# A softmax-by-polynomial step moved from VectorE to GpSimd, in an order planned with the cost of both engines' shared accesses

## The chip, the cores and the metric

The kernel runs on one core of a Trainium2 chip. A core has a matrix engine (TensorE, PE in the profile), a vector engine (VectorE, DVE), a scalar engine for exponentials (ScalarE, ACT), a general engine (GpSimd, POOL) and a queue engine (SyncE, SP) that here only starts DMAs. Each works through its own list of instructions in order; semaphores order the engines among each other. On-chip memory is SBUF, and PSUM (eight banks) for what TensorE writes. The metric is the device time in microseconds of one execution, the median of several runs.

## The reference

Two attention blocks share the input `x` (1 x 2048 x 512) and are mixed by a gate. Block A is softmax attention with 32 heads of 16 dimensions; block B is linear attention with a learned feature map.

```python
g = sigmoid((x * gate_w).sum(-1, keepdims=True))
# A: softmax attention, 32 heads, Dh = 16
scores = einsum("bhqd,bhkd->bhqk", q, k) * Dh ** -0.5
a = (softmax(scores) @ v) @ A_wo
# B: feature maps by softmax over 16 features, both signs
phi_q = concat(softmax(pq), softmax(-pq)); phi_k = concat(softmax(pk), softmax(-pk))
kv = einsum("bhsf,bhsd->bhfd", phi_k, v); z = phi_k.sum(s)
b = ((phi_q @ kv) / (phi_q @ z + 1e-6)) @ B_wo
return g * a + (1 - g) * b
```

Block A needs 32 x 2048 x 2048 exponentials. That is 2048 tiles of 128 x 512 (128 keys by 512 queries of one head).

## The kernel before, in words

**Tiles.** Four tiles (four heads that lie in the four quarters of TensorE's rows) are a pack, and there are 512 packs. Sixteen packs, one for each block of 128 keys, are a group: one accumulator bank in which the four heads' values and the sums of the exponentials (a column of ones beside the values) build up. Eight groups cover 512 queries.

**Two ways to an exponential.** Most tiles go the short way. TensorE makes the scores of three or two tiles at a time (`_qk`) into a ring of five PSUM banks, ScalarE makes the exponentials of the three or two with one instruction (`_exp`, line 1035) into 25 slots `ET`, and TensorE multiplies them with the values (`_pv`, line 1104). Other tiles, "away", are made by VectorE (`_vector_batch`). It makes 2 to the power of the scaled score by hand, for batches of up to five tiles, in six steps:

1. `v_bits`, line 883, once a tile: the scores of the tile, a bank of PSUM, are scaled and written as unsigned integers to `vt`, so that the bits hold exponent and fraction.
2. `_frac`, line 907, once a batch: one byte of every word of `vt` becomes a 16-bit fraction in `vf`.
3. `_line`, line 909: a linear form of `vf` in `vu`.
4. `_sq`, line 910: `vf` squared.
5. `_cube`, line 911: `vu` times `vf`.
6. `v_out`, line 893: `vt`, scaled, plus `vu`, written as 16-bit words that are the exponentials in bfloat16.

There are two buffers `vt`, one `vf` and three `vu`. The tiles are then multiplied with the values by TensorE, one at a time (`pvx`). `SHARES` says for each of the 32 groups how many of its tiles are away, and `_plan_vector` spreads them over the packs of the group by an integer division; the two tiles of each of the first two batches (`SOON`) come on top.

**The rest of the work.** VectorE also takes what TensorE made out of PSUM (projections of q, k and v, lines 703, 759, 783; block B's projections, lines 1252 and 1268; finished output rows, lines 1489 and 1541), turns each accumulator (line 1157), divides by the sum (lines 1161 to 1169), and makes block B's feature maps (lines 1306 to 1365). GpSimd only sets constants at the start; its last instruction begins at 25.84 us. SP starts the DMAs, among them eight small ones per q projection that spread heads (line 761).

**The order.** Nothing of the order is left to the engines. The kernel makes a list of operations (`Plan.op`) with an engine, a cost in microseconds, dependencies, a priority (often a date, counted in packs) and an earliest date. `Plan.order` walks through time, keeps when each engine is free, takes the operation that can start first (among those within 0.02 us the one of least priority), hands out spare PSUM banks (three beside the ring; one of them holds the accumulator), and adds filling matmuls on zeros (line 1113) where TensorE would be idle too long. The result is each engine's list; `emit` writes it with the semaphore waits that the dependencies need. So each engine's list is fixed by the costs in the code, and where the chip differs from them an engine waits at its list's head while what stands behind it waits too.

Names that matter for the change: `LEAD` (how many packs ahead of its first use a batch is due), `VPRIO`, `VREL`, `QDUE`, `K0`, `SK`, `Q0`, `SQ` (dates of batches, q projections, and block B's parts), `FIRST` and `LAST` (sizes of the first and last batches), `ENDS` (where the last group's away tiles lie), `OREL` (earliest date of the last outputs).

## Time and profile before

| | |
|---|---|
| time, median of 3 runs | 838.03 us (837.74 to 838.34) |
| profiled execution: span from first to last instruction | 836.5 us; the page has no other time of it |
| TensorE busy | 792.9 us (95%), of it fills 255.3 us |
| VectorE busy | 806.8 us (96%), 1050 instructions |
| ScalarE busy | 825.4 us (99%), of it exponentials 823.1 us |
| GpSimd busy | 8.0 us (1%), all within the first 26 us |
| granted TensorE clock | 1.000 |

How to read it: the page gives for each engine the time in which it worked on some instruction, as a share of the span. Its groups put together instructions of one line, engine and operation: the output, the input and their shapes, how many there were, the busy time and the mean duration of one in ns, and then how long the engine had been idle just in front of them and who ended that. Durations of neighbours on an engine can overlap a little, so count times mean can be more than the busy time. A row of the table of waits has who waited, for whom, and in total how long, how many times, and the longest.

### The profile page before, as it was taken

The page shows a single profiled execution, that of the slowest core. Times are in us where ns is not written, and L with a number is a line of the kernel's source. Part 1 is how long each engine was busy: PE and PEld are TensorE (multiplying, and loading weights), DVE is VectorE, ACT ScalarE, POOL GpSimd, SP SyncE. Part 2 cuts the span into 40 slices and gives each one's busy share as a digit, 9 for nine tenths or more (in the row PEclk, how much of TensorE's full clock was granted, in tenths as well). Part 3 has the DMA queues.
Part 4 walks back from the last instruction along what each step waited for, and adds up shares of the span by engine and source line. Part 5 has one row for each costly group of instructions (what it writes and reads, how often), then busy time and mean ns, then how long its engine had stood idle before and what let it go on. Part 6 is the DMA issues. An engine that isn't in the chain of part 4 may idle for free.

```text
span 836.5 us, 19540 instructions
## 1 busy us (share of the span) xinstructions
PE 792.9 (95%) x8711; PEld 263.0 (31%) x8753; DVE 806.8 (96%) x1050; ACT 825.4 (99%) x733; POOL 8.0 (1%) x15
## 2 busy tenths in 40 slices
PE   9999999999999999999999999999999999999998
PEld 4323333333232222232223322222322223222234
DVE  6999999999999999999999999999998999999994
ACT  7999999999999999999999999999999999999997
POOL 3000000000000000000000000000000000000000
PEclk9999999999999999999999999999999999999999
DMA  9500000000000000210003010003100003000000
GB/s 250 157 6 8 1 7 1 2 1 8 2 7 2 7 1 8 52 22 13 1 7 59 20 33 2 4 5 70 27 15 8 1 11 79 21 8 2 2 2 27
DMA packets 49027, 20.01 MB, mean 24 GB/s; under 512 B 38704, under 2 KB 48944, under 8 KB 48944
## 3 DMA queue, kind: packets, MB, share of 16 engines
q1 hardware_dynamic: 48272, 18.58, 9.4%
q8 instruction: 68, 1.11, 0.6%
q10 hardware_dynamic: 672, 0.20, 0.1%
q14 instruction: 15, 0.12, 0.0%
HBM read 6.31 MB, written 2.10 MB: 10 GB/s over the span
## 4 chain that ended last, share of the span: by engine, by line
ACT 92%; DVE 5%; PE 2%; DMA 0%; SPq 0%; issue 0%
ACT ET L1035 92%; DVE vt L883 1%; PE ps L984 0%; DMA qT<-qraw 0%; SPq L761 0%; PE ps L633 0%; DVE vu L893 0%; PE ps L1113 0%; DVE bq L1268 0%; DVE vt L1321 0%; DVE VB L1252 0%; DVE T L1157 0%; DVE vf L907 0%; DVE vu L911 0%; DVE vf L910 0%; DVE bq L1315 0%
## 5 line engine op out<-in xcount | busy, mean ns | idle before, releaser
L1035 ACT ACTIVATE ET<-ps 128x1536 bf16<-128x1536 f32 x728 | 823.1, 1397 | 1.7 <-PE ps L984 1.5
L984 PE MATMUL ps<-qT,kT 32*128 32x512 bf16 (+2 forms) x2249 | 318.4, 364 | 31.4 <-ACT ET L1035 22.2
L1113 PE MATMUL ps<-kT,zero 128*32 128x512 bf16 (+1 forms) x3052 | 255.3, 383 | 0.0
L1104 PE MATMUL ps<-ET,V 128*32 128x512 bf16 (+2 forms) x1998 | 195.8, 364 | 1.3 <-ACT ET L1035 0.6
L984 PEld LDWEIGHTS ps<-qT,kT 32*128 32x128 bf16 x2249 | 83.5, 91 | 305.5 <-ACT ET L1035 227.1
L883 DVE TENSOR_SCALAR vt<-ps 128x512 uint32<-128x512 f32 x226 | 148.3, 681 | 3.8 <-PE ps L984 3.1
L893 DVE SCALAR_TENSOR_TENSOR vu<-vt,vu 128x2560 int16<-128x2560 uint32 (+3 forms) x47 | 127.6, 2716 | 0.7
L1113 PEld LDWEIGHTS ps<-kT,zero 128*32 128x32 bf16 x3052 | 67.9, 94 | 103.2 <-issue 78.5
L1104 PE MATMUL ps<-vu,V 128*32 128x512 bf16 (+1 forms) x250 | 85.3, 364 | 0.3 <-DVE vu L893 0.3
L1104 PEld LDWEIGHTS ps<-ET,V 128*32 128x32 bf16 x1998 | 55.0, 95 | 67.0 <-issue 36.9
L910 DVE TENSOR_TENSOR vf<-vf 128x2560 f16<-128x2560 f16 (+3 forms) x49 | 68.6, 1400 | 0.6
L911 DVE TENSOR_TENSOR vu<-vu,vf 128x2560 f16<-128x2560 f16 (+3 forms) x49 | 68.5, 1398 | 0.5
L907 DVE TENSOR_SCALAR vf<-vt 128x2560 f16<-128x2560 uint8 (+3 forms) x47 | 67.1, 1427 | 0.2
L681 PE MATMUL ps<-WB,xT 128*128 128x512 bf16 x165 | 48.8, 383 | 4.0 <-issue 1.6
L909 DVE TENSOR_SCALAR vu<-vf 128x2560 f16<-128x2560 f16 (+3 forms) x49 | 37.9, 774 | 2.0 <-PE ps L1104 1.8
L681 PE MATMUL ps<-xT,WA 128*128 128x512 bf16 (+1 forms) x124 | 35.8, 380 | 0.0
L1157 DVE STREAM_TRANSPOSE T<-ps 128x512 f32<-128x512 f32 (+1 forms) x35 | 23.2, 664 | 5.0 <-PE ps L1104 4.6
L1104 PEld LDWEIGHTS ps<-vu,V 128*32 128x32 bf16 x250 | 22.9, 96 | 11.5 <-issue 8.5
L681 PEld LDWEIGHTS ps<-WB,xT 128*128 128x128 bf16 x192 | 14.4, 97 | 27.0 <-issue 14.3
L1268 DVE TENSOR_SCALAR bq<-ps 128x512 bf16<-128x512 f32 x32 | 21.5, 679 | 0.5 <-PE ps L681 0.4
L777 PE MATMUL ps<-WA,xT 128*128 128x128 bf16 x256 | 18.9, 220 | 0.4 <-DVE vt L883 0.2
L1321 DVE TENSOR_TENSOR vt<-vt,brec 128x4096 bf16<-128x4096 bf16 (+1 forms) x10 | 18.6, 1857 | 0.0
(105 smaller groups left out, 421.8 us busy)
## 6 DMA issues: line engine op xcount, KB each, us to landing
qT<-qraw SPq DMA_DIRECT2D x120, 16.0 KB, 1.8
xn<-in_A_x_dram SPq DMA_DIRECT2D x3, 512.0 KB, 6.1
WB<-in_B_wqkv_dram SPq DMA_DIRECT2D x3, 512.0 KB, 5.0
out_dram<-WB SPq DMA_DIRECT2D x12, 128.0 KB, 1.9
WA<-in_A_wqkv_dram SPq DMA_DIRECT2D x3, 384.0 KB, 5.2
xn<-in_A_x_dram SPq DMA_DIRECT2D x2, 256.0 KB, 3.6
WoA<-in_A_wo_dram SPq DMA_DIRECT2D x1, 512.0 KB, 5.7
WoB<-in_B_wo_dram SPq DMA_DIRECT2D x1, 512.0 KB, 6.6
```

What stands on the lines that cost most here:

```text
L681: mm = op("PE", lambda e, c=c: e.matmul(self._bank(job)[:, 0:n], lhs(c), rhs(c), start=(c == 0), stop=(c == 3)), self.c_pe(n), reads=reads ...
L883: parts.append(op("DVE", lambda e, j=j, job=job: e.tensor_scalar(vt[:, j, :], self._bank(job), SCALE * LOG2E * 2.0 ** 24, 2.0 ** 31, op0=A ...
L893: o = op("DVE", lambda e: e.scalar_tensor_tensor(out=flat(vu).bitcast(I16), in0=flat(vt), scalar=2.0 ** -17, in1=flat(vu), op0=ALU.mult, o ...
L907: ("_frac", two, lambda e: e.tensor_scalar(vf, frac, 1 / 256, ROOT, op0=ALU.mult, op1=ALU.add), [b_vt], [b_vf]),
L909: lambda e: e.tensor_scalar(vu, vf, CUBE, SQUARE, op0=ALU.mult, op1=ALU.add), [b_vf], [b_vu]),
L910: ("_sq", two, lambda e: e.tensor_tensor(vf, vf, vf, ALU.mult), [b_vf], [b_vf]),
L911: ("_cube", two, lambda e: e.tensor_tensor(vu, vu, vf, ALU.mult), [b_vf, b_vu], [b_vu]),
L984: ins = e.matmul(out[u][:, cols], self.kT[32 * i:32 * i + 32, cp, kt * TOK:(kt + 1) * TOK], self.qT[32 * i:32 * i + 32, s, q], start=True, ...
L1035: o = plan.op("ACT", lambda e: e.activation(self.ET[:, a % NS:a % NS + n, :], self.ps[:, a % NR:a % NR + n, :], ACT.Exp, scale=SCALE), sel ...
L1104: ins = e.matmul(self._bank(ot)[32 * i:32 * i + 32, to], self.V[:, kt, g8 // 2, v0:v0 + 32], tile[:, cols], start=first and j == 0, stop=o ...
L1113: ins = e.matmul(self._bank(ot)[32 * i:32 * i + 32, lo:QCH], self.zero[:], self.kT[:, 0, lo:QCH], start=False, stop=False, tile_position=( ...
L1157: return e.transpose(to, acc if alone else acc.rearrange("p (e b d) -> p e b d", e=2, b=8))
```

## The change

The fraction step (`_frac`) of the batches goes from VectorE to GpSimd, except in the first two batches (the `SOON` tiles) and the last two. There it is cut in pieces of at most three tiles: a batch of five is a piece of three and a piece of two. Each piece depends on the reads (`v_bits`) of its own tiles, on the last readers of `vf`, and on the `v_out` made last.

The planner gets a rule for what it calls the port: a set of names, which holds VectorE's steps between SBUF and SBUF (steps 2 to 6 above, block B's feature maps, parts of the division) and the pieces on GpSimd. An instruction of the set on one of the two engines doesn't begin before the other engine's last one of the set has ended, plus 0.1 us (GpSimd after VectorE) or 0.12 us (VectorE after GpSimd). VectorE doesn't start one that would begin less than 0.25 us before the next piece that GpSimd could start. Each such order becomes a dependency, hence a semaphore wait. VectorE's reads of PSUM aren't in the set. A piece's planned cost is 0.165 us and 0.00084 us per element.

TensorE may score into the banks for a tile buffer once `_cube` of the buffer's earlier batch is done, where it waited for the buffer's last reader; the read `v_bits` itself now waits for the last readers.

The shares are new (they add up to 246 where they added up to 226), the last group has ten away tiles where it had seven (spread over 11 places where it was 9). The rest batch stays in front of the last. Dates get a correction for each batch (`EASE`, `HURRY`), each q projection (`QEASE`), each part of block B (`LEASE`) and each output tile (`OEASE`), and several general dates are changed.

```diff
+        self.port = name in Plan.PORT
...
+    PORT = {"v_frac", "v_line", "v_sq", "v_cube", "v_out", "gate_z", "gate_h", "gate_b", "n_den", "n_mul", "kvbd", "b_grid", "b_rest",
+            "b_max", "b_top", "b_octave", "b_square", "b_slope", "b_even", "b_odd", "b_part", "b_out", "b_sum", "b_ratio", "b_mul"}
+    GUARD, GIVE, TAKE = 0.25, 0.1, 0.12
...
+            pool = [(max(free["POOL"], o.dep_t, port["DVE"].end + self.GIVE if port["DVE"] else 0.0), o) for o in avail["POOL"]
+                    if o.port and o.rel <= self.now]
+            booked = min(pool, key=lambda x: x[0]) if pool else None
...
+                    if o.port and e == "POOL" and port["DVE"]:
+                        t = max(t, port["DVE"].end + self.GIVE)
+                    elif o.port and e == "DVE":
+                        if port["POOL"]:
+                            t = max(t, port["POOL"].end + self.TAKE)
+                        if booked and t > booked[0] - self.GUARD:
+                            t = max(t, booked[0] + booked[1].cost + self.TAKE)
...
+            if o.port and e in port:
+                other = port["DVE" if e == "POOL" else "POOL"]
+                if other is not None:
+                    o.deps.append(other)
+                port[e] = o
...
-    QDUE, VPRIO, VREL, TPRIO = 28.0, -16.0, 161.0, 5
-    KEEP = 14
+    NVT, PIECE = 2, 3
+    QDUE, VPRIO, VREL, TPRIO = 32.287, -12.758, 161.0, 1
+    KEEP = 15
...
-    OREL = 3
-    ENDS = 9
+    OREL = 0
+    ENDS = 11
+    POOL = 0.00084
+    SOONER = "_cube"
+    TAIL = 2
...
-    SHARES = (0, 2, 2, 6, 0, 5, 4, 5, 8, 4, 9, 9, 10, 4, 15, 4,
-              2, 14, 8, 8, 12, 3, 6, 7, 14, 8, 7, 12, 6, 11, 14, 7)
+    SHARES = (0, 2, 4, 6, 2, 0, 5, 5, 16, 0, 9, 13, 4, 13, 11, 3, 11, 13, 6, 9, 9, 6, 12, 4, 11, 11, 8, 5, 12, 12, 14, 10)
...
-            due = max(units[0] / 4 - self.LEAD, self.EARLY if 2 * k >= len(soon) else self.SDUE)
+            due = max(units[0] / 4 - self.LEAD + self.EASE[k], self.EARLY if 2 * k >= len(soon) else self.SDUE)
...
-                   reads=self._score_bufs([u]), deps=b_vt.readers, name="vqk", prio=due + step * j, rel=due + step * j - self.VREL, kind="row",
+                   reads=self._score_bufs([u]), deps=b_vt.soon or b_vt.readers, name="vqk", prio=due + step * j, rel=due + step * j - self.VREL, kind="row",
...
-                op0=ALU.mult, op1=ALU.add), self.c_dve(512), deps=[m], name="v_bits",
+                op0=ALU.mult, op1=ALU.add), self.c_dve(512), deps=[m, *b_vt.readers], name="v_bits",
...
-        prio = units[0] / 4 - self.VPRIO
+        prio = units[0] / 4 - self.VPRIO + self.HURRY[number]
...
-            op("DVE", fn, cost, reads=reads, writes=writes, name="v" + name, prio=prio)
-        o = op("DVE", lambda e: e.scalar_tensor_tensor(
+            if name == "_frac" and not soon and number < len(self.batches) - self.TAIL:
+                o = self._frac(vt, vf, parts, b_vt, b_vf, prio)
+            else:
+                o = op("DVE", fn, cost, reads=reads, writes=writes, name="v" + name, prio=prio)
+            if name == self.SOONER:
+                b_vt.soon = [o]
+        self.last_out = o = op("DVE", lambda e: e.scalar_tensor_tensor(
...
+    def _frac(self, vt, vf, parts, b_vt, b_vf, prio):
+        free, made, at = b_vf.readers or b_vf.writers, [], 0
+        while at < len(parts):
+            n = min(self.PIECE, len(parts) - at)
+            made.append(self.plan.op(
+                "POOL", lambda e, a=at, n=n: e.tensor_scalar(
+                    vf[:, a:a + n, :], vt[:, a:a + n, :].bitcast(U8).rearrange("p n (q h) -> p n q h", h=4)[:, :, :, 2], 1 / 256, ROOT,
+                    op0=ALU.mult, op1=ALU.add), 0.165 + n * QCH * self.POOL, deps=[*parts[at:at + n], *free, self.last_out],
+                name="v_frac", prio=prio))
+            at += n
+        b_vt.readers += made
+        b_vf.writers, b_vf.readers = made, []
+        return made[-1]
...
-    K0, SK, Q0, SQ = 17.0, 8.5, 178.25, 18.0
+    K0, SK, Q0, SQ = 17.036, 8.76, 176.771, 19.0477
...
-            due = max(128 * (qc + 1) + 8, self.Q0 + self.SQ * (4 * qc + 4) + 22) + 4 * tt
+            due = max(128 * (qc + 1) + 8, self.Q0 + self.SQ * (4 * qc + 4) + 22) + 4 * tt + self.OEASE[t]
```

More of the change, by code (lines that the diff above doesn't have):

```diff
@@ L32, in __init__ @@
         self.readers = []
+        self.soon = []
 class Job:
@@ L81 @@
     LATE = 9.5
+    PORT = {"v_frac", "v_line", "v_sq", "v_cube", "v_out", "gate_z", "gate_h", "gate_b", "n_den", "n_mul", "kvbd", "b_grid", "b_rest",
+            "b_max", "b_top", "b_octave", "b_square", "b_slope", "b_even", "b_odd", "b_part", "b_out", "b_sum", "b_ratio", "b_mul"}
+    GUARD, GIVE, TAKE = 0.25, 0.1, 0.12
+    MOVE = {}
     def __init__(self):
@@ L94, in op @@
            acquire=None, release=None, lat=None, array=None, groups=None):
+        if name in self.MOVE:
+            eng, cost = "POOL", self.MOVE[name](cost)
         o = Op(eng, fn, cost, name, prio, rel, kind, self.LAT[eng] if lat is None else lat, groups)
@@ L165, in order @@
         queues = {e: [] for e in self.ENGS}
+        port = {"DVE": None, "POOL": None}
         left = len(self.ops)
@@ L383 @@
     LAST = (4,)
-    OREL = 3
-    ENDS = 9
+    OREL = 0
[3 more added lines that the diff above has]
+    TAIL = 2
+    REST = 48
+    HURRY = (0, 9.6, 3.1, -5.4, 16.2, -6.1, 0, -3.2, 10.5, 1.0, -8.4, 1.5, -3.1, 0.6, 12.0, 0, 9.6, 12.6, 0, -8.4, 6.7, 11.7,
+              7.3, 0.7, -7.6, 2.9, 0.1, 0, 3.9, 0.3, 13.7, 4.0, 0, 3.9, -14.1, -5.6, -2.1, 7.4, 4.3, -1.8, -2.7, 18.1, -9.4,
+              5.8, 4.8, 3.9, -6.0, 0, 0, 0, 0, 0, 0, 0, 0, 0, 0, 0, 0, 0)
+    QEASE = (0, 4.2, -1.3, -2.9, 5.7, 0.3, 9.3, 7.6, 5.5, 9.6, -1.4, -2.2, -1.6, 9.1, 3.3, 2.1)
+    LEASE = (-2.3, 3.2, 8.7, -2.0, 0, -20.0, -1.6, -2.5, -9.6, -3.3)
+    OEASE = (-0.2, -4.3, 8.5, -1.3, 2.6, -5.0, 14.2, -2.3, 10.6, -2.1, 6.7, 3.8, 0.9, 0, 0, 0)
+    EASE = (0, -0.9, 0, 6.0, -3.1, 3.7, 3.4, 3.9, 4.6, -1.9, -1.0, 0.1, 12, 8.0, 5.5, -12.1, -3.2, 8.6, 12, 9.8, 0, -1.0, -9.5,
+              -3.3, -14, 0, 9.6, -2.8, -0.4, -10.7, 0, 10.0, -8.8, 5.2, -5.7, -4.3, -10.6, 0, -0.6, -3.0, 9.6, 3.5, -3.4, 12,
+              12, -14, -4.8, 0, -0.2, 4.8, 0, -4.5, -1.6, 0, 0, 4.2, 0, 0, 0, 0)
+    NBANK = 8
     def __init__(self, nc, A_x, A_wqkv, A_wo, B_wqkv, B_w_phi, B_wo, gate_w, out):
@@ L403, in build @@
             p.pad = lambda ot: lambda e: self._fill(e, ot)
-            p.free_banks = [(b, 0.0, []) for b in range(self.NRING, 8)]
+            p.free_banks = [(b, 0.0, []) for b in range(self.NRING, self.NBANK)]
             self._loads()
@@ L439, in _memory @@
         self.xn = sb("xn", [P, NT, D], BF16)
-        at[0] = max(at[0], xn_at + 2 * self.NB * QCH * 4)
-        self.vt = nc.alloc_sbuf_tensor_at("vt", [P, 2, self.NB, QCH], I32U, offset=xn_at)
+        at[0] = max(at[0], xn_at + self.NVT * self.NB * QCH * 4)
+        self.vt = nc.alloc_sbuf_tensor_at("vt", [P, self.NVT, self.NB, QCH], I32U, offset=xn_at)
         self.xT = sb("xT", [P, NT, 4, TOK], BF16)
@@ L752, in _proj_q @@
         n = qc * 4 + cp
-        due = 32 * n - self.QDUE
+        due = 32 * n - self.QDUE + self.QEASE[n]
         s0 = 2 * (n % (self.NQS // 2))
@@ L844, in _plan_vector @@
         left = len(self.away) - sum(self.FIRST) - sum(self.LAST)
-        sizes = [*self.FIRST, *[self.NB] * (left // self.NB), *[left % self.NB] * (left % self.NB > 0), *self.LAST]
+        sizes = [self.NB] * (left // self.NB)
+        sizes[self.REST:self.REST] = [left % self.NB] * (left % self.NB > 0)
+        sizes = [*self.FIRST, *sizes, *self.LAST]
         ends = [sum(sizes[:k + 1]) for k in range(len(sizes))]
@@ L865, in _vector_batch @@
         NB = len(units)
-        k, slot, soon = self.n_bits % 2, number % self.NVU, 2 * number < len(self.SOON)
+        k, slot, soon = self.n_bits % self.NVT, number % self.NVU, 2 * number < len(self.SOON)
         self.n_bits += not soon
@@ L884, in _vector_batch @@
                 vt[:, j, :], self._bank(job), SCALE * LOG2E * 2.0 ** 24, 2.0 ** 31,
-                op0=ALU.mult, op1=ALU.add), self.c_dve(512), deps=[m], name="v_bits",
+                op0=ALU.mult, op1=ALU.add), self.c_dve(512), deps=[m, *b_vt.readers], name="v_bits",
                 prio=due + step * j - 40, release=job))
-        b_vt.writers, b_vt.readers = parts, []
+        b_vt.writers, b_vt.readers, b_vt.soon = parts, [], []
         self.last_bits = parts
         n = NB * QCH
-        prio = units[0] / 4 - self.VPRIO
+        prio = units[0] / 4 - self.VPRIO + self.HURRY[number]
         for name, cost, fn, reads, writes in self._cubic(flat(vt), flat(vf), flat(vu), n, b_vt, b_vf, b_vu):
-            op("DVE", fn, cost, reads=reads, writes=writes, name="v" + name, prio=prio)
-        o = op("DVE", lambda e: e.scalar_tensor_tensor(
+            if name == "_frac" and not soon and number < len(self.batches) - self.TAIL:
[5 more added lines that the diff above has]
+        self.last_out = o = op("DVE", lambda e: e.scalar_tensor_tensor(
             out=flat(vu).bitcast(I16), in0=flat(vt), scalar=2.0 ** -17, in1=flat(vu), op0=ALU.mult, op1=ALU.add),
@@ L918, in _attention @@
         self.n_bits = 0
+        self.last_out = None
         self._plan_vector()
@@ L925, in _attention @@
         self.b_outt = [Buf() for _ in range(6)]
-        self.b_vt, self.b_vf, self.b_vu = [Buf() for _ in range(2)], Buf(), [Buf() for _ in range(self.NVU)]
+        self.b_vt, self.b_vf, self.b_vu = [Buf() for _ in range(self.NVT)], Buf(), [Buf() for _ in range(self.NVU)]
         for b in self.b_vt:
@@ L1199, in _branch_b @@
             if t < self.PAIRS or t % 4 == 0:
-                due = self.K0 + self.SK * t
+                due = self.K0 + self.SK * t + self.LEASE[len(self.linear)]
                 self.linear.append((due, lambda t=t, due=due: self._b_keys(t, 2 if t < self.PAIRS else 4, due)))
         for t in range(0, NT, 4):
-            due = self.Q0 + self.SQ * t
+            due = self.Q0 + self.SQ * t + self.LEASE[len(self.linear)]
             self.linear.append((due, lambda t=t, due=due: self._b_queries(t, due)))
@@ L1274, in _b_part @@
             x.writers, x.readers = list(parts), []
-        k, n, h, ng = self.n_bits % 2, 2 * nt * QCH, nt * QCH, 16 * nt
+        k, n, h, ng = self.n_bits % self.NVT, 2 * nt * QCH, nt * QCH, 16 * nt
         self.n_bits += 1
         b_vt, b_vf = self.b_vt[k], self.b_vf
+        b_vt.soon = []
         two, four = lambda n: 0.057 + n * 0.000525, lambda n: 0.066 + n * 0.000262
```

## The prediction

> **What bounds the kernel now.** I read the engine totals first, then the costliest groups, then ScalarE's waits, then VectorE and GpSimd by shape, then VectorE in stretches of 50 us and in order of time. The head of the page and two of its groups:

> ```profile
> span 836.5 us, 19540 instructions
> PE 792.9 (95%) x8711; PEld 263.0 (31%) x8753; DVE 806.8 (96%) x1050; ACT 825.4 (99%) x733; POOL 8.0 (1%) x15
> ...
> L1035 ACT ACTIVATE ET<-ps 128x1536 bf16<-128x1536 f32 x728 | 823.1, 1397 | 1.7 <-PE ps L984 1.5
> ...
> L1113 PE MATMUL ps<-kT,zero 128*32 128x512 bf16 (+1 forms) x3052 | 255.3, 383 | 0.0
> ```

> ScalarE runs exponentials for 823.1 of 836.5 us and idles 1.7 us in front of them. The list of all that it ever waited for is short:

> ```profile
> ACT kT L721 <- PE ps L715: 3.7, 1, 3.7
> ACT xT L1544 <- PE ps L1531: 2.2, 1, 2.2
> ACT ET L1035 <- PE ps L984: 1.5, 3, 0.7
> ```

> (total, times, longest.) The exponentials start at 7.35 us, end at 831.64 us by order of time, and 4.9 us of last tile, eviction and store follow. So the time is a head, the exponentials and a tail: only fewer exponentials shorten it, as long as the others keep up. TensorE has room, by the table of waits:

> ```profile
> PEld ps L984 <- ACT ET L1035: 227.1, 510, 1.0
> PEld ps L1113 <- issue: 78.5, 324, 0.4
> ```

> It waits 227.1 us for ScalarE in front of the scores, and the 3052 matmuls of L1113 only fill. VectorE has hardly any: between 20 and 800 us its busy times by stretch add up to 768.7 of 780, 11.3 us idle. The granted clock is 1.00 in every stretch. VectorE's batch of five tiles, by shape (count | busy, mean ns):

> ```profile
> L883 DVE TENSOR_SCALAR vt<-ps 128x512 uint32<-128x512 f32 x226 | 148.3, 681 | 3.8 <-PE ps L984 3.1
> L893 DVE SCALAR_TENSOR_TENSOR vu<-vt,vu 128x2560 int16<-128x2560 uint32 x43 | 121.2, 2818 | 0.6
> L910 DVE TENSOR_TENSOR vf<-vf 128x2560 f16<-128x2560 f16 x43 | 63.7, 1482 | 0.5
> L911 DVE TENSOR_TENSOR vu<-vu,vf 128x2560 f16<-128x2560 f16 x43 | 63.6, 1479 | 0.4
> L907 DVE TENSOR_SCALAR vf<-vt 128x2560 f16<-128x2560 uint8 x43 | 63.6, 1478 | 0.2
> L909 DVE TENSOR_SCALAR vu<-vf 128x2560 f16<-128x2560 f16 x43 | 35.0, 813 | 2.0 <-PE ps L1104 1.8
> ```

> L907 is the step that moves. These durations overlap by about 0.08 us; what counts is the distance from start to start, read in order of time:

> ```profile
> 726.02 0.82 DVE L909 TENSOR_SCALAR vu<-vf 128x2560 f16<-128x2560 f16 x1
> 726.87 1.49 DVE L910 TENSOR_TENSOR vf<-vf 128x2560 f16<-128x2560 f16 x1
> 728.28 1.88 DVE L883 TENSOR_SCALAR vt<-ps 128x512 uint32<-128x512 f32 x3
> 730.08 1.48 DVE L911 TENSOR_TENSOR vu<-vu,vf 128x2560 f16<-128x2560 f16 x1
> 731.59 2.82 DVE L893 SCALAR_TENSOR_TENSOR vu<-vt,vu 128x2560 int16<-128x2560 uint32 x1
> ```

> That is 1.40 us for a product, 0.60 for one PSUM read of L883 (1.80 for three), 2.74 for L893 (start to next start), 0.74 to 0.85 for L909; L907 to its successor is 1.40 too.

> The sum is made against the profiled execution: its span of 836.5 us is all the page has of its own time; the median of the three runs, 838.03, stands 1.5 us above it, and I carry that 1.5 over.

> **The change, part by part.**

> *Tiles taken from ScalarE.* The shares add up to 226 before and 246 after, with 4 early tiles on top. But the formula of the places names a tile twice where a share is larger than the 14 places: a share of 15 in 14 before (one twice), 16 in 14 after (two twice). Distinct tiles: 229 before, 248 after. The trace agrees: 222 value matmuls of full width plus 7 last tiles in 4 blocks is 250, the count of L1104 from vu. ScalarE keeps 2048 - 248 = 1800 tiles instead of 1819: by shape it now has 364 threes, 363 twos and 1 one, afterwards 360 and 360. The planner's cost, 0.0642 us + 0.000833 per element, gives 822.8 us for what the row says is 823.1, so I use it: 4 threes (1.344), 3 twos (0.917) and 1 one (0.491) are **8.6 us less**. On the path in full, since the exponentials are the path.

> *VectorE's load.* Freed: L907 in all batches but the first two early ones and the last two: 43 x 1.40, and about 3.2 for the small ones, less 2.0 for the last batches of three and four that stay: 61.4 us. Added: 20 tiles (the second copies are made as well) of 0.60 for the read and (0.74 + 1.40 + 1.40 + 2.74)/5 = 1.26 for the rest: 37.1 us. Net 24.3 us freed. With the 11.3 us idle, and 8.6 us less span to do it in, VectorE can stand still for 27.0 us more than now before it is late: 49 batches go through GpSimd, so **0.55 us a batch**; 0.73 us a batch before the whole gain is gone (35.6/49).

> *GpSimd's pieces.* 47 batches of five in pieces of three and two, two batches of two: 96 pieces, at the end of a queue that is empty after 26 us. No trace shows this operation there. The nearest rows:

> ```profile
> L571 POOL MEMSET qT<- 128x2048 bf16 x1 | 1.8, 1804 | 0.0
> ...
> L574 POOL TENSOR_TENSOR wphi<-wphin,heads 128x512 bf16<-128x512 bf16 x1 | 1.1, 1051 | 1.5 <-DMA wphin<-in_B_w_phi_dram 1.5
> L791 POOL MEMSET gwb<- 128x544 bf16 x1 | 0.6, 631 | 0.0
> L1192 POOL MEMSET kvbd<- 128x544 bf16 x1 | 0.6, 552 | 0.0
> ```

> The memsets give 0.153 + 0.000806 per element (0.592 at 544, 1.804 at 2048): 1.39 and 0.98, 2.37 us a batch, as the low end (they read nothing). The product, with two inputs, has 2.05 ns an element: 3.15 and 2.10, 5.25 us, the high end. One input and a 2-byte output are nearest to the memset; the planner's 1.455 and 1.025, 2.48 us, lie beside it, and I take 2.48.

> *The waits that come with it.* A piece waits for the reads of its own two or three tiles, for the last L893 and, by the new rule of ports, for VectorE's last instruction of the port set; VectorE's next port instruction waits for the piece, and in its queue everything behind it does: the reads that free banks for TensorE, hence scores, hence ScalarE. A handover took 0.03 us in the trace (GpSimd's iden to VectorE's mask) and 0.06 (VectorE's onTA to TensorE); the planner's 0.1 and 0.12 are the upper bound: 2.48 + 0.22 = 2.70 us a batch. What hides it: instructions that read PSUM. The five L883 of another batch are 3.0 us, and they can start at the same L893 that lets the piece start. In all there are 148 us of L883 and, from their rows, some 147 of other non-port work (transposes, casts, evictions, reciprocals) against 49 x 2.70 = 132. If the cover holds, the cost is a few tenths a batch and inside the 0.55: nothing on the path. Bounds: 0 to 2.70 us a batch.

> *Scores released sooner, other dates.* TensorE may score for a tile buffer after the cube instead of L893; it takes a bank up to 2.7 us earlier and shortens the wait after L893. The 20 more single score and value passes are, with the planner's 0.213 and 0.104 for a switch, at most 12.7 us, in the place of fills (3052/4 x 0.213 = 163 us): nothing. The new dates of projections, branch B and stores, SP's 120 qT copies with them, move work that lies beside the exponentials; only head and tail could show it. The head has none of it; the last group has ten tiles instead of seven, and now two in the very last block, in the same batch of four that the block before needs: 0 to 1 us, taken as 0.

> *Sum.* 838.0 - 8.6 = 829.4; and 1.0 us for ScalarE's new small waits, an estimate: now 1.7 us with one supplier, and VectorE now has two sources of delay; between 0 and 4. **830.4 us.**

> **The rivals.**

> *VectorE waits for GpSimd (slower).* Two spare PSUM banks must turn over every 0.6 us to give five reads in a row; the longest run in the stretch shown is three (1.80 us), and elsewhere single reads lie between port instructions, which can't any more. With three as cover, a batch waits 2.70 - 1.80 = 0.90 us: 829.4 + 49 x (0.90 - 0.55) = **846.6**. It decides from 0.73 us a batch on. For it: 98.6% of VectorE is taken; between packs 256 and 384 the tiles go from 60 to 70, by which VectorE gains nothing (10 x 1.86 against 60 x 0.28). Against it: the work outside the port set, 295 us, is twice what is needed, and later tiles have slots for three batches. [...]

> *A part of the cover fails.* A wait of 0.65 us a batch: 829.4 + 49 x 0.10 = **834.3**, still faster.

> *GpSimd at the product's rate.* 5.47 us a batch with 3.0 covered: 829.4 + 49 x (2.47 - 0.55) = **923**. Against it: the step has one input.

> *ScalarE doesn't get shorter in effect:* the tiles go but dates misfit and ScalarE waits as long as it gained, **838**; for it only that VectorE's margin is small.

> **How the numbers follow.** Forecast case (827.5 to 832) 0.52; part of the cover 0.18; about as before 0.05; VectorE late 0.22 and GpSimd at the product's rate 0.03. What can be told from no change is about 0.2%, 1.7 us. Faster 0.70, same 0.05, slower 0.25. The low end is 829.4 less ScalarE's 1.7 us of waits, rounded: 827.5. Up to 842 the range takes in the partial case, no change and the mild third of the late case (a wait of 0.81 us a batch); what is left out above holds 0.18, below 0.03.

> **What would show it.** ScalarE: 720 exponentials, 814 us, waits below 5 us. GpSimd: 96 pieces near 1.45 and 1.0 us. VectorE: busy near 782 us, and waits on GpSimd below 27 us in all; if they pass 36 us, the forecast falls. If pieces last 2 us and more, the product's row was the right one. If ScalarE waits on TensorE while TensorE waits on VectorE's reads, the late case is here.

## The result and the profile after

The changed kernel takes 832.97 us, the median of four runs (830.17 to 833.76), against 838.18 us: a ratio of 0.9931 (95% interval 0.9915 to 0.9947). It is faster, by 5.2 us of the 7.6 that were forecast, and inside the range (827.5 to 842), which also held no change and a slower kernel. The profiled execution took 832.89 us, with a span of 831.0. In the head of its page and in its groups, the lines that answer to those of before (L1095 is the exponentials, L1173 the fills, L952 the pieces on GpSimd):

```profile
span 831.0 us, 19239 instructions
PE 799.8 (96%) x8526; PEld 263.4 (32%) x8526; DVE 785.8 (95%) x1041; ACT 817.2 (98%) x725; POOL 127.0 (15%) x111
...
PEclk9999999999979999999999999999999999999999
...
L1095 ACT ACTIVATE ET<-ps 128x1536 bf16<-128x1536 f32 x720 | 814.9, 1371 | 4.4 <-PE ps L1044 3.8
...
L1173 PE MATMUL ps<-kT,zero 128*32 128x512 bf16 (+1 forms) x2824 | 236.5, 386 | 0.0
```

Exponentials went from 823.1 to 814.9 us (728 to 720 instructions), ScalarE's idle time in front of them from 1.7 to 4.4 us. Those two account for the span: -8.2 + 2.7 = -5.5. The head (first exponential at 7.29 us, before 7.35) and the tail (4.9 us after the last one, as before) are the same.

GpSimd's pieces, by shape, and what VectorE waited for, by the table of waits (total, times, longest):

```profile
L952 POOL TENSOR_SCALAR vf<-vt 128x1536 f16<-128x1536 uint8 x47 | 69.2, 1471 | 605.0 <-DVE vu L938 360.7 <-DVE vt L923 154.8 <-DVE bq L1399 89.5
L952 POOL TENSOR_SCALAR vf<-vt 128x1024 f16<-128x1024 uint8 x49 | 51.2, 1045 | 46.4 <-DVE vt L923 41.7 <-DVE vu L938 4.7
```

```profile
DVE vt L923 <- PE ps L1044: 12.3, 24, 1.2
...
DVE vu L968 <- POOL vf L952: 2.9, 6, 0.6
...
DVE bq L1395 <- POOL vf L952: 0.9, 1, 0.9
...
DVE WB L1396 <- POOL vf L952: 0.4, 1, 0.4
...
DVE vt L1367 <- POOL vf L952: 0.2, 1, 0.2
```

A piece of three tiles takes 1.47 us and one of two 1.05, and VectorE waits for the pieces 4.4 us in the whole run, 9 times. How one batch is covered shows in order of time (start, length, engine, line and operation; in brackets the idle time just before, and what ended it):

```profile
563.11 1.22 DVE L923 TENSOR_SCALAR vt<-ps 128x512 uint32<-128x512 f32 x2
...
563.82 2.52 POOL L952 TENSOR_SCALAR vf<-vt 128x1536 f16<-128x1536 uint8 x2 [28.17 <-DVE vt L923]
...
564.52 2.51 DVE L923 TENSOR_SCALAR vt<-ps 128x512 uint32<-128x512 f32 x4 [0.19 <-PE ps L1044]
...
566.94 0.28 DVE L1425 TENSOR_TENSOR brec<-bsum,brec 128x128 f16<-128x128 f32 x1
567.14 0.82 DVE L968 TENSOR_SCALAR vu<-vf 128x2560 f16<-128x2560 f16 x1
```

Both pieces end at 566.34 us, beside six reads of PSUM in a row, and VectorE's next instruction of the port set comes 0.6 us later.

What was not forecast is the 7 in the line of TensorE's clock. In stretches (columns: the stretch, its length, busy time and instructions of PE, PEld, DVE, ACT and POOL in this order, granted clock, DMA share, GB/s):

```profile
200.00:228.00 28.00, 27.16 (x275) 7.70 (x277) 27.03 (x30) 28.00 (x26) 2.48 (x2) 1.00 0.02 5
228.00:234.00 6.00, 3.76 (x29) 0.97 (x21) 5.90 (x7) 6.00 (x7) 0.00 (x0) 0.91 0.03 6
234.00:244.00 10.00, 9.70 (x74) 2.56 (x75) 8.88 (x11) 7.48 (x8) 2.48 (x2) 0.54 0.01 2
...
780.00:790.00 10.00, 8.97 (x104) 3.06 (x96) 9.00 (x13) 8.99 (x9) 2.48 (x2) 0.83 0.01 2
```

TensorE has little to do for about four microseconds (busy 2.75 of the 4.96 us up to 232.96), then works at a granted clock of 0.50 for some ten (232.96 to 243.20), and ScalarE loses 2.5 us there, and 1.0 us near 785. These 3.5 us are most of its 4.4 us of waits. What TensorE and VectorE do ahead of it:

```profile
226.84 0.11 PEld L1044 LDWEIGHTS ps<-qT,kT 32*128 32x128 bf16 x2 [0.39 <-DVE vu L970]
227.04 2.82 DVE L938 SCALAR_TENSOR_TENSOR vu<-vt,vu 128x2560 int16<-128x2560 uint32 x1
...
227.60 0.83 PE L1173 MATMUL ps<-kT,zero 128*32 128x512 bf16 x12
...
228.25 0.39 PE L1164 MATMUL ps<-ET,V 128*32 128x512 bf16 x4
...
229.78 1.75 DVE L1417 RECIPROCAL brec<-bsum 128x256 f16<-128x256 f32 x1
...
230.88 0.39 PE L1044 MATMUL ps<-qT,kT 32*128 32x512 bf16 x3 [0.95 <-ACT ET L1095]
...
231.44 6.58 DVE L923 TENSOR_SCALAR vt<-ps 128x512 uint32<-128x512 f32 x10
...
237.48 1.04 PE L1164 MATMUL ps<-ET,V 128*32 128x512 bf16 x7 [0.18 <-DVE vt L923]
```

The matmuls at 228.25 are the last value products of a group of packs; until 237.48 there are no fills and no value products, only scores. Just ahead, at 226.84, stand two scores for VectorE, which the cube (L970) let go: they may come early now. They hold both spare banks until VectorE has done L938 and the reciprocal and reads them from 231.44 on; so the next group gets no accumulator, and without one the planner has nowhere to put fills. This is read from the list and the trace; no run takes back the early scores alone. A second part of the change bears on the same place: `KEEP`, the pack of a group from which the planner keeps a bank back for the next accumulator, went from 14 to 15 (of 0 to 15), so that only the group's last pack, which stands behind the two scores, does it. Which of the two changes makes the gap, or whether it takes both, isn't shown.

### The profile page after: what moved, and what is told of

The parts are those of the page before. It is cut to its first block, busy times and chain, and to the rows that moved or that the text cites. A ratio compares the mean times of both kernels' runs of the same rounds, so it can differ in the third digit from the quotient of the medians.

```text
span 831.0 us, 19239 instructions
## 1 busy us (share of the span) xinstructions
PE 799.8 (96%) x8526; PEld 263.4 (32%) x8526; DVE 785.8 (95%) x1041; ACT 817.2 (98%) x725; POOL 127.0 (15%) x111
## 4 chain that ended last, share of the span: by engine, by line
ACT 72%; DVE 20%; PE 6%; POOL 1%; issue 0%; DVEq 0%
ACT ET L1095 72%; DVE vu L938 3%; DVE vt L923 2%; PE ps L1044 2%; DVE vu L970 1%; DVE vf L969 1%; PE ps L1164 1%; DVE bq L1328 1%; POOL vf L952 1%; DVE VB L1312 1%; PE ps L1173 1%; DVE vt L1382 1%; DVE vu L968 1%; DVE bq L1420 1%; PE ps L720 1%; DVE V L822 1%
## 5 line engine op out<-in xcount | busy, mean ns | idle before, releaser
L1095 ACT ACTIVATE ET<-ps 128x1536 bf16<-128x1536 f32 x720 | 814.9, 1371 | 4.4 <-PE ps L1044 3.8
L1044 PE MATMUL ps<-qT,kT 32*128 32x512 bf16 (+2 forms) x2250 | 322.5, 367 | 25.0 <-ACT ET L1095 17.3
L1173 PE MATMUL ps<-kT,zero 128*32 128x512 bf16 (+1 forms) x2824 | 236.5, 386 | 0.0
L952 POOL TENSOR_SCALAR vf<-vt 128x1536 f16<-128x1536 uint8 (+1 forms) x96 | 118.9, 1254 | 651.4 <-DVE vu L938 365.4
L1164 PE MATMUL ps<-ET,V 128*32 128x512 bf16 (+2 forms) x1970 | 196.8, 368 | 1.0 <-DVE T L1217 0.5
L1044 PEld LDWEIGHTS ps<-qT,kT 32*128 32x128 bf16 x2250 | 85.8, 91 | 305.6 <-ACT ET L1095 203.0
L923 DVE TENSOR_SCALAR vt<-ps 128x512 uint32<-128x512 f32 x246 | 159.7, 680 | 14.8 <-PE ps L1044 12.3
L938 DVE SCALAR_TENSOR_TENSOR vu<-vt,vu 128x2560 int16<-128x2560 uint32 (+3 forms) x51 | 138.8, 2721 | 0.6
L1173 PEld LDWEIGHTS ps<-kT,zero 128*32 128x32 bf16 x2824 | 62.5, 95 | 98.9 <-issue 77.4
L1164 PE MATMUL ps<-vu,V 128*32 128x512 bf16 (+1 forms) x278 | 92.4, 364 | 0.1
L969 DVE TENSOR_TENSOR vf<-vf 128x2560 f16<-128x2560 f16 (+3 forms) x53 | 74.5, 1405 | 0.5
L970 DVE TENSOR_TENSOR vu<-vu,vf 128x2560 f16<-128x2560 f16 (+3 forms) x53 | 74.4, 1404 | 0.5
L1164 PEld LDWEIGHTS ps<-ET,V 128*32 128x32 bf16 x1970 | 54.7, 96 | 60.1 <-issue 32.4
L720 PE MATMUL ps<-WB,xT 128*128 128x512 bf16 x192 | 56.6, 383 | 0.6
L1164 PEld LDWEIGHTS ps<-vu,V 128*32 128x32 bf16 x278 | 24.7, 96 | 19.3 <-issue 14.5
```

Source lines behind the costliest of these rows:

```text
L720: mm = op("PE", lambda e, c=c: e.matmul(self._bank(job)[:, 0:n], lhs(c), rhs(c), start=(c == 0), stop=(c == 3)), self.c_pe(n), reads=reads ...
L923: parts.append(op("DVE", lambda e, j=j, job=job: e.tensor_scalar(vt[:, j, :], self._bank(job), SCALE * LOG2E * 2.0 ** 24, 2.0 ** 31, op0=A ...
L938: self.last_out = o = op("DVE", lambda e: e.scalar_tensor_tensor(out=flat(vu).bitcast(I16), in0=flat(vt), scalar=2.0 ** -17, in1=flat(vu), ...
L952: "POOL", lambda e, a=at, n=n: e.tensor_scalar(vf[:, a:a + n, :], vt[:, a:a + n, :].bitcast(U8).rearrange("p n (q h) -> p n q h", h=4)[:, ...
L969: ("_sq", two, lambda e: e.tensor_tensor(vf, vf, vf, ALU.mult), [b_vf], [b_vf]),
L970: ("_cube", two, lambda e: e.tensor_tensor(vu, vu, vf, ALU.mult), [b_vf, b_vu], [b_vu]),
```

## The experiments

**The changed kernel again, and the same order with fills added.** The second kernel differs by this alone:

```diff
+            more = {**{f"qk{k}": 2 for k in range(196, 202)}, **{f"qk{k}": 1 for k in (*range(202, 205), *range(679, 685))}}
+            for o in p.queues["PE"]:
+                o.filled += more.get(o.name, 0)
```

> The changed kernel once more, to see how its time and the granted clock go together. If the time lost against 829.4 us is the clock's, the runs with a mean clock of 0.99 lie at 832.5 to 834 us and those with 0.996 or more at 830.5 or less; if VectorE's lateness is the cause, time and clock don't go together.

> The order of the changed kernel, with 21 filling matmuls more in two places (two ahead of each of the scores 196 to 201, one ahead of 202 to 204 and of 679 to 684, in the bank that these scores then write). Clock theory: the granted clock stays at 1.00 through 232 to 243 us and 780 to 790 us, ScalarE's waits for L1044 and L1164 fall from 4.3 to about 1 us, the time to 829.0 to 830.2 us. Rival, VectorE is late there and the low clock only goes with it: the clock is 1.00, but ScalarE still waits 3.5 to 4.5 us and the time stays at 832 to 833.5 us.

The changed kernel took 833.52 us (0.9943, 0.9929 to 0.9957): 831.70 at a mean clock of 0.994, 831.34 at 0.993, 833.52 at 0.991, 833.74 and 833.85 at 0.990. With the first four (830.17 at 0.996, then 832.89, 833.06 and 833.76 at 0.990 to 0.991) time and clock go together, as expected. The run at 0.994 only seems slower than the one at 0.993: their spans are 829.2 and 829.5 us. The profiled execution here is the one at 0.994. In it the clock falls in the first gap alone; from 780 to 790 us it is 1.00 and ScalarE works all 10 us, where it lost 1.0 us before.

With the 21 fills it took **830.01 us** (829.96 to 830.19; 0.9906, 0.9893 to 0.9920), with a clock of 1.00 in each run. Stretches and waits of that kernel:

```profile
228.00:234.00 6.00, 4.94 (x34) 1.11 (x26) 5.64 (x6) 5.77 (x6) 0.00 (x0) 1.00 0.02 5
234.00:244.00 10.00, 9.67 (x114) 3.59 (x116) 9.70 (x14) 9.73 (x10) 2.48 (x2) 1.00 0.01 2
...
780.00:790.00 10.00, 9.43 (x121) 3.34 (x121) 9.25 (x15) 10.00 (x10) 2.48 (x2) 1.00 0.01 2
```

```profile
ACT ET L1098 <- PE ps L1047: 1.2, 3, 0.7
```

More work on TensorE made the kernel 3.0 us faster than in its first runs and 3.5 faster than in the runs made together with these. VectorE does what it did (785.7 us, the same waits on GpSimd), and it still comes late with its reads, so its lateness isn't the cause; the clock is. Part of the wait is not: 228 to 244 us still has 0.5 us without exponentials.

**Another order without the gap.** 31 dates differ, of which for example:

```diff
-    QDUE, VPRIO, VREL, TPRIO = 32.287, -12.758, 161.0, 1
+    QDUE, VPRIO, VREL, TPRIO = 31.856, -16.838, 161.0, 1
...
-    K0, SK, Q0, SQ = 17.036, 8.76, 176.771, 19.0477
+    K0, SK, Q0, SQ = 17.036, 8.76, 176.384, 19.0477
```

and entries of `HURRY`, `EASE`, `QEASE`, `LEASE` and `OEASE`.

> The changed kernel with 31 of its dates different (dates of batches, q projections, block B's parts and outputs) and all else as it was, so that the order is a new one: it has the same tiles on each engine, but a stretch without fills such as the one near 230 us isn't in it. No fill is added by hand. If missing matmuls are what the changed kernel loses by, the granted clock is 1.00 throughout, ScalarE waits less than 2 us in front of its exponentials, and the time is 829.4 to 830.6 us with little spread; if the 21 added fills helped in another way, the time is 832 to 834 as for the changed kernel.

830.22 us (0.9914, 0.9900 to 0.9928). The six values again show what the clock is worth: 829.35, 829.55 and 829.91 at 1.00, 830.53 and 830.82 at 0.998, 833.48 at 0.994. So the clock is not 1.00 throughout in three of six runs, and the spread is larger than expected; where it falls in them isn't shown, as the profiled execution is one at 1.00. In that one ScalarE waits 1.1 us for scores, and TensorE is busy 11.97 of the 12 us from 228 to 240:

```profile
228.00:240.00 12.00, 11.97 (x154) 4.46 (x152) 11.85 (x16) 12.00 (x11) 2.64 (x3) 1.00 0.01 3
```

An order with the same tiles and no gap does as well as the fills, if not as steadily.

**A gap made in the kernel before.**

```diff
+            q = p.queues["PE"]
+            for o in [o for o in q if 423 <= o.start < 441]:
+                if o.name == "pad":
+                    q.remove(o)
+                o.filled = 0
```

> The kernel before, order kept, with the filling matmuls left out in one stretch of some 18 us (planned at 423 to 441 us, on the chip near 427 to 445). It has no change in it and VectorE isn't late. If a lack of matmuls alone lowers the clock, it goes from 1.00 to about 0.5 in that stretch, ScalarE's waits rise from 1.7 us by 1 to 4 us and the time to 839 to 842 us; if the low clock came from something else in the change, the clock stays at 1.00 and the time at 838.

840.68 us (1.0032, 1.0020 to 1.0044), as expected, with mean clocks of 0.986 to 0.990. By stretch, first the kernel before with its fills, then without:

```profile
424.00:448.00 24.00, 22.71 (x267) 6.46 (x266) 23.90 (x39) 24.00 (x23) 0.00 (x0) 1.00 0.03 7
```

```profile
424.00:428.00 4.00, 3.20 (x24) 0.87 (x21) 4.00 (x10) 4.00 (x5) 0.00 (x0) 1.00 0.00 0
428.00:432.00 4.00, 2.85 (x18) 0.52 (x16) 4.00 (x8) 4.00 (x4) 0.00 (x0) 0.70 0.00 0
432.00:436.00 4.00, 2.94 (x21) 0.56 (x18) 4.00 (x7) 4.00 (x5) 0.00 (x0) 0.50 0.05 12
436.00:440.00 4.00, 3.44 (x22) 0.72 (x22) 4.00 (x6) 4.00 (x4) 0.00 (x0) 0.50 0.08 21
440.00:444.00 4.00, 3.84 (x25) 0.59 (x21) 4.00 (x7) 4.00 (x5) 0.00 (x0) 0.50 0.00 0
444.00:448.00 4.00, 4.00 (x29) 0.61 (x25) 2.92 (x7) 3.04 (x3) 0.00 (x0) 0.50 0.02 4
448.00:452.00 4.00, 4.00 (x42) 1.10 (x40) 2.46 (x3) 2.65 (x3) 0.00 (x0) 0.74 0.45 84
```

Without the fills the clock falls to 0.50 within some 6 us and stays there for about 20. From 428 to 444 us, at 0.70 and 0.50, ScalarE is busy throughout; then it loses 2.3 us in eight (444 to 452), as TensorE is full (4.00 of 4.00) at 0.50 and 0.74. A lack of matmuls is enough; nothing of the change is needed.

**The port order taken away.** All waits between port instructions of the two engines go, and the pieces' wait for L938 (`side` is the other engine's instruction that the rule put among the dependencies):

```diff
+            for o in p.ops:
+                if o.side is not None:
+                    del o.deps[max(i for i, d in enumerate(o.deps) if d is o.side)]
+                if o.eng == "POOL" and o.name == "v_frac":
+                    o.deps = [d for d in o.deps if d.name != "v_out"]
```

> The changed kernel's order of every engine, without the semaphore waits that keep the port instructions of the two engines apart, and without the pieces' wait for the last L938 (what the data need is still waited for). Pieces can then start as soon as their tiles are read, beside products and L938. If the two engines exclude each other, pieces that lasted 1.47 and 1.05 us or the L938 of 2.82 us get longer by what they overlap (means up by 0.3 us or more), and the time is the same or worse, 832 to 842 us. If they don't, all durations stay, the waits on GpSimd fall from 4.4 us to under 1 us, and the time is 829 to 833 us.

844.36 us (1.0077, 1.0056 to 1.0097): slower than both kernels, and above the 842 expected at most. Pieces by shape, VectorE's last step (L945 here, 2.815 us before the edit), and one overlap in order of time:

```profile
L959 POOL TENSOR_SCALAR vf<-vt 128x1536 f16<-128x1536 uint8 x47 | 120.5, 2564 | 524.7 <-DVE vu L977 245.4 <-DVE vt L930 189.7 <-DVE bq L1406 89.6
L959 POOL TENSOR_SCALAR vf<-vt 128x1024 f16<-128x1024 uint8 x49 | 88.0, 1797 | 47.6 <-DVE vt L930 44.6 <-DVE vu L977 3.0
```

```profile
L945 DVE SCALAR_TENSOR_TENSOR vu<-vt,vu 128x2560 int16<-128x2560 uint32 x47 | 145.1, 3088 | 0.6
```

```profile
579.40 5.04 POOL L959 TENSOR_SCALAR vf<-vt 128x1536 f16<-128x1536 uint8 x2 [6.95 <-DVE vu L977]
...
579.84 3.71 DVE L945 SCALAR_TENSOR_TENSOR vu<-vt,vu 128x2560 int16<-128x2560 uint32 x1
```

The pieces and L945 last longer in this run: means of 2.56, 1.80 and 3.09 us, where 1.47, 1.05 and 2.82 were. In this overlap the piece of three runs from 579.40 to 580.87, in its 1.47 us. L945 comes up in the middle of it, takes 0.89 us longer than its 2.82 and ends at 583.55. The piece of two is recorded from 580.84 to 584.45, 3.61 us, of which 0.90 lie behind the end of L945, near the 1.05 that it takes in the changed kernel. Where L945 starts first, at 259.15 us, it keeps its 2.83 us, and the piece of three beside it takes 4.11. So in both of these overlaps the instruction that started first kept its length. Beside reads of PSUM in the same run, at 569.98 us, two pieces take 2.48 us. The overlap at 579.40 buys next to nothing (5.05 us for the three instructions, 5.34 one after the other), and overlaps come at moments that the order didn't plan: ScalarE waits 11.7 us, and the mean clock was 0.984 to 0.989. How much of the 11 us is the one and how much the other wasn't separated.

**A longer time on GpSimd.** One more one-tile piece behind 45 batches:

```diff
+                x = Op("POOL", self.longer(o), 0.59, "v_more", 0.0, -99, "full", 0.12)
+                x.deps = [d for d in (o, last) if d is not None]
+                q.insert(q.index(o) + 1, x)
+                for u in p.ops:
+                    if u is not x and u.eng == "DVE" and o in u.deps:
+                        u.deps.append(x)
```

> The order of the changed kernel, with one more one-tile piece (0.59 us by the pieces' rates) on GpSimd behind 45 of the 49 batches' pieces; it writes a spare buffer and VectorE's next port instruction waits for it too. From the trace, 15 of the batches have VectorE's next port instruction within 0.1 us of the piece's end and the median margin is some 0.4 us; 0.6 to 0.7 us more should make VectorE wait some 17 us more. Cover theory (little margin): waits on GpSimd go from 4.4 to 18 to 25 us, ScalarE's waits rise, 837 to 846 us. Rival, GpSimd has room: below 834 us.

847.22 us (1.0111, 1.0097 to 1.0124), just above the expected range. The 45 added pieces take 0.62 us each. VectorE's waits on GpSimd, of which these are the largest, went from 4.4 to 21.4 us, as expected:

```profile
DVE vu L988 <- POOL gwb L962: 12.2, 18, 1.3
...
DVE WB L1416 <- POOL gwb L962: 2.3, 2, 1.6
...
DVE bq L1415 <- POOL gwb L962: 1.6, 1, 1.6
```

17 us more of waiting made the kernel about 14 us slower. GpSimd is 18% busy and has no room: its place in the order has none.

**The fraction step back on VectorE.** The order of the changed kernel, each piece moved into VectorE's list just ahead of its batch's linear step, and the port rule's waits that name a piece left out:

```diff
+            for o in moved:
+                pool.remove(o)
+                o.eng = "DVE"
+                dve.insert(next(i for i, x in enumerate(dve) if x.name == "v_line" and o in x.deps), o)
```

> The changed kernel's tiles, dates and order, but each piece of the fraction step runs on VectorE, just ahead of the linear step of its batch. VectorE gets 47 x 1.46 + 2 x 0.60 = 70 us back, against 31.6 us that it now idles between 20 and 800 us, of which some 10 us are waits for scores that the order can't give back. Budget theory: VectorE sets the time, ScalarE waits 30 to 70 us, 860 to 900 us. Rival, only the number of ScalarE's tiles counts: 833 us.

925.0 us, in a single run, and beyond the range. VectorE's busy time rose by 73.8 us to 859.6, near the 70 that were worked out, but it is idle for 63 us, 22.4 of it for scores, ScalarE waits 78 us for scores, and the mean clock is 0.943. So ScalarE's fewer tiles alone don't make the gain: VectorE's load decides. That the delays feed on themselves (late reads, no banks, gaps on TensorE, a granted clock of 0.89 from 200 to 400 us) is the likely reason for the surplus over 900, but no run separates its parts.

**The old shares with the new step.** The old `SHARES` and the old `ENDS`, 9, in the changed kernel, ordered anew.

> The changed kernel with the shares and the last group of the kernel before (229 distinct tiles, ScalarE keeps 1819), the fraction step on GpSimd as changed, ordered anew with the same rules and dates. If the gain is that of the tiles alone, ScalarE's exponentials take 823 us again and the time is 837 to 841 us although VectorE has some 60 us less to do; if the move to GpSimd is worth something by itself, the time is below 836 us.

842.74 us (1.0054, 1.0037 to 1.0071), above the expected range. ScalarE's row is back at 823.9 us, as expected, and VectorE has 753.0 us to do:

```profile
L1096 ACT ACTIVATE ET<-ps 128x1536 bf16<-128x1536 f32 x728 | 823.9, 1389 | 5.9 <-PE ps L1045 3.8
```

VectorE idles 88 us and ScalarE still waits 5.9 us: the dates belong to the other tiles, and VectorE waits 19.3 us on GpSimd and once 10.2 us for a value product. Relief for VectorE alone is worth nothing here; what it would be worth with dates of its own stays open.

## Why the prediction was right, point by point

- *Tiles taken from ScalarE, 8.6 us*: right. 720 exponentials, 8.2 us less, and the time follows them.
- *GpSimd's pieces, 2.48 us a batch, the planner's price, just above the memsets' 2.37*: right, 1.47 + 1.05 = 2.52; the product's price of 5.25 is out, and with it the 923 us.
- *The cover*: right in the main, VectorE waits 4.4 us on GpSimd, below 27 and far from 36. But VectorE's idle time between 20 and 800 us rose from 11.3 to 31.6 us, so 20.3 of the 27.0 us that I had as allowance are used. Near half of the rise is waits for scores (3.1 to 12.3 us at L883, now L923; 6 times before, 24 now): to read five banks in a row VectorE now waits for TensorE more often, and longer in all, than for GpSimd (9 times, 4.4 us). The experiment with longer pieces fits this count: 17 us more wait, less the 6.7 left, should cost 10; it cost 14. The late rival was thus closer than its 0.73 us a batch made it look. By the number alone, 832.97, the case in which part of the cover fails (834.3) lies nearer than the forecast sum (830.4); the 4.4 us of waits, and 830.01 us once the gaps are filled, speak against it.
- *VectorE's load, 24.3 us freed*: the way is right, the size is 3.3 us off: 785.8 us busy, 21.0 less, where I had near 782. No run says where the 3.3 us lie.
- *Fills, "in the place of fills ...: nothing"*, and *scores released sooner*, which were only to shorten a wait: this is the step that failed. The fills are not slack to be spent. Two early scores held both banks at a group's end, no fill could be placed, and the clock fell; that the missing fills cost the time is shown, what in the change let the scores in is read from list and trace.
- *1.0 us for ScalarE's new small waits*: mis-sized, it was 2.7 us, and in the main not for the reason given (two sources of delay at VectorE). With the two gaps filled it is 0.1 us (1.8 in place of 1.7), and the time of 830.01 us is then 0.6 above the sum without this term, 829.4.
- *The port order, counted as handovers of 0.22 us a batch*: the forecast took it as the planner has it, and the trace of the kernel before couldn't show what it is for, as GpSimd is empty after 26 us there. Without it the pieces of three and L945 take 2.56 and 3.09 us on average, where 1.47 and 2.82 were, and the kernel 844.36; with it VectorE waits for GpSimd 4.4 us in all.

## What to carry to other kernels

Where one engine is full, count what leaves its list, and then ask of every other engine whether it still gets its work in time: here the first gave the size to half a microsecond. Matmuls that only fill are part of the schedule; after any reordering, look at the granted clock by stretch, not at its mean, which hides a gap of ten microseconds behind 0.99. An engine that is mostly idle can be full where it matters: GpSimd at 15% had under half a microsecond between a batch's last piece and VectorE's next port instruction in most batches.
